# Attention, a gated MoE and a SwiGLU on one core: when the next stage's blocks are loaded and split, and when stores are issued

## The chip, the core and the metric

One core of one Trainium2 chip. The metric is the device time of one execution, in microseconds, as the median of several runs. TensorE is PE, VectorE is DVE, ScalarE is ACT, GpSimd is POOL; SP is the sync engine, whose queue issues nearly all of the DMAs here, strictly in program order: an entry that waits holds all entries behind it.

## The reference

Three parts follow one another; every output token depends on all three.

```python
k_p = k.reshape(B, H, Sp, 8, D).mean(3); v_p = ...           # B, H, S, D = 4, 8, 576, 64
attn = softmax(q @ k_p.T / sqrt(D)); x = (attn @ v_p)        # 2304 tokens x 512
p = domain_probs / domain_probs.sum(-1)
x = sum over e of p[:, e] * (relu(x @ w1[e]) @ w2[e])        # E = 4, 512 x 1024
xn = x / sqrt(mean(x * x) + 1e-6) * rms_g
out = (silu(xn @ w_gate) * (xn @ w_val)) @ w_out             # 512 x 1536
```

## The kernel before

The 2304 tokens are worked in three passes `p` of six tiles of 128 (TT = 6). A pass has an "m" part (4 experts x 4 rows of weights) and a "gv" part (6 rows of gate and value). The order is six **stages**: m0, m1, m2, then gv0, gv1, gv2; a stage of type m has 16 **quads**, one of type gv has 12 (`g`, `v` in turn). `quads` (L147) is the list, `stages` (L739) groups it, and `ids` are the quads of the stage in hand.

**A quad** (L286) multiplies the stage's x (512 x 768, cut in four blocks a11, a12, a21, a22 of 256 x 384) by a 2 x 2 block of weights with seven block products instead of eight (`STEPS`, L42). Each product is six matmuls: every float32 operand is split into a high part (an ACT copy to float32r) and a low part (a DVE subtraction), and high x high, high x low and low x high are added in PSUM (L304 to L306). X, Y and Z are the PSUM banks; after steps 0 to 2 ACT copies a bank away (`s`, L309), after steps 3 to 5 DVE adds (`u` L311 and L313, `v` L315). PE's next product into the same bank has to wait for that reader.

**x_ops** (L104) makes the seven operands of x for a stage: four DVE additions (L118), seven high parts on ACT (L111) and seven low parts on DVE (L115), into tiles `xo...` that have one buffer each, and so can be written only when the old stage's last quad has read them. `load_x` (L89) loads the four blocks from DRAM (`xs_d`), all at the end of the second-to-last quad (L822); `x_ops` is spread over the last quad from its step 2 on (L790) and over the first two steps of the new stage. For the early stages the blocks borrow the buffers `rw`, `tw`, `kr`, `vr`.

**The hook** (L776) runs after each step and hands out side work, in this order: the quad's own epilogue, a share of `second` (the second matmuls, L391: three matmuls a unit, two units a step in the m stages, one in the gv stages), the next quad's weights (`prep_w`, L175, and `prep_w2`, L227), `xit` (x_ops), `norms`, one piece of `convert_all` (L245), one entry of the attention's list (`att_step`). In the first stage and in gv0 the weights come raw, are combined on POOL (L193 to L197), split on ACT and DVE and stored to DRAM (`wr_d` L204, `wt_d` L212, `w2_d` L242); in later stages `prep_w` only loads them again (L186, L187). Raw blocks are loaded by `load_w` (L172) and `load_w2` (L224).

**norm** (L435) takes the MoE's result of a pass: for each of six tiles it loads y from DRAM (L449) into a buffer `st`, three steps later scales it (L453), two steps later transposes it on PE (L458), copies it to another `st` (L460), and stores it to `xs_d` (`store_x`, L87). `second` stores y with L420.

**Attention.** The first pass's six tiles come before the first quad, in the loop at L664 and in the order 0, 3, 1, 4, 2, 5: `att_a` is the scores (L556), maximum (L565), and eight exponentials on ACT (L568); `att_b` scales by the sums (L575 to L577); `att_c` transposes (L585) and copies to `aT` (L587); `att_d` multiplies by v (L599) and copies to x (L607). After every second tile `x_ops` runs on its part of x. The other tiles are handed out by steps during m0 and m1 (L712), the last of a stage ending at its step 95 of 112.

Of the kernel before, what the change touches and what calls it, by code (L numbers as in the profile page):

```python
# [53 lines left out]
def tile_kernel(ctx: ExitStack, tc, qp, kp, vp, dp, w1r, w2r, w64, rg, out):  # L54
# [34 lines left out]
    def load_x(kind, p, early):  # L89

        tags = (("rw", main), ("tw", main), ("kr", sba), ("vr", sba))
        for n, (o, d) in enumerate(((0, 0), (N, 0), (0, 1), (N, 1))):
            if early:
                tag, pool = tags[n]
                t = pool.tile([P, 4 * 256], F32, name="xr", tag=tag)[:, :2 * N]
            else:
                t = late["cv"].tile([P, 2 * N], F32, name="xr", tag=f"x{n}")
            t = t.rearrange("p (c n) -> p c n", c=2)
            nc.sync.dma_start(t, xs_d[kind, p, d, :, :, o:o + N])
            xr[o, d] = t  # L100

    xo = {}

    def x_ops(c0=0, c1=N, new=True):  # L104
# [16 lines left out]
        high("a11", a11)  # L121
        high("s3", a21)
        low("a11", a11)
# [13 lines left out]
        low("s1", a11)  # L137
        yield
        low("a12", a12)
        add(a12, a21, ALU.subtract)  # L140
# [23 lines left out]
    raw, wop = {}, {}  # L164

# [9 lines left out]
    def prep_w(i):  # L175
# [28 lines left out]
        nc.sync.dma_start(wr_d[n], wrf)  # L204
# [7 lines left out]
        nc.sync.dma_start(wt_d[n], wtf)  # L212
        yield
# [13 lines left out]
    def prep_w2(key):  # L227
        t = main.tile([P, 2, 2, DM], F32R, name="w2", tag="w2", bufs=4)
        w2[key] = t
        k, p, e, row = key  # L230
        d = w2_d[place2(k, e, row)]
        tf = f32(t).rearrange("p a s n -> p (a s n)")
        if p:
            nc.sync.dma_start(tf, d)
            return
        r = raw2.pop(key)
        for c in range(2):
            nc.scalar.activation(t[:, 0, c], r[:, c], AF.Copy)
            yield
            nc.vector.tensor_tensor(t[:, 1, c], r[:, c], f32(t[:, 0, c]), op=ALU.subtract)  # L240
            yield
        nc.sync.dma_start(d, tf)  # L242
# [148 lines left out]
    def second(keys, first, last):  # L391

        k, p, e, _ = keys[0]
        for t in (3, 4, 5, 0, 1, 2):
# [18 lines left out]
            elif k == "m":  # L413
                nc.vector.scalar_tensor_tensor(y_t[t], ps, gate, y_t[t], op0=ALU.mult, op1=ALU.add)  # L414
                if last:
# [4 lines left out]
                    nc.sync.dma_start(y_d[p, t], y_t[t])  # L420
# [14 lines left out]
    def norm(p):  # L435
# [10 lines left out]
        yield  # L446
        for t in range(TT):
            y = stage().rearrange("p d n -> p (d n)")
            nc.sync.dma_start(y, y_d[p, t])  # L449
            yield  # L450
            yield
            yield
# [7 lines left out]
            nc.scalar.activation(st, ps.rearrange("p (d n) -> p d n", d=ND), AF.Copy)  # L460
            store_x(1, p, t, st)
# [85 lines left out]
    def att_a(i):  # L547
# [5 lines left out]
        for j in range(NPAIR):  # L553
            o = (j % 2) * 2 * SP
            for p0, n, b in parts(i):
                nc.tensor.matmul(  # L556
                    sc[p0:p0 + n, j // 2, o:o + 2 * SP], q[:, j, p0:p0 + n],
                    kpb[b % 2][:, j].rearrange("p a s -> p (a s)"), start=True, stop=True,
                )
# [4 lines left out]
        scale = 1.0 / (POOL * math.sqrt(D))  # L564
        nc.vector.tensor_reduce(m.rearrange("p (a h) -> p a h", a=2), v, axis=AX.X, op=ALU.max)  # L565
# [5 lines left out]
        es_t[i] = es, sm  # L571

# [6 lines left out]
    def att_c(i):  # L579
# [6 lines left out]
        for a in range(2):  # L586
            nc.scalar.activation(aT[:, 4 * a:4 * a + 4, :], tr[a][:SP, :].rearrange("p (h s) -> p h s", h=4), AF.Copy)  # L587
# [56 lines left out]
    ]  # L644
    next(k0[0])
    next(k0[1])
    load_q(order[0])
# [16 lines left out]
    for n in range(TT + 2):  # L664
        if n >= 2:
            att_c(order[n - 2])
        if n < TT:
            att_a(order[n])
# [11 lines left out]
        if 1 <= n <= TT:  # L680
            att_b(order[n - 1])
# [85 lines left out]
    for si, ((moe, p), ids) in enumerate(stages):  # L767
        done = []
        for i in ids:
# [6 lines left out]
            def hook(n, u, v, x):  # L776
# [13 lines left out]
                if i != ids[-1] or n >= 2:  # L790
                    run(xit)
                run(norms)
# [8 lines left out]
            if i == ids[-1] and si + 1 < len(stages):  # L801
                xit.append(x_ops())
# [19 lines left out]
            if i == ids[-2] and si + 1 < len(stages):  # L822
                m2, p2 = stages[si + 1][0]
                load_x(0 if m2 else 1, p2, si < 2)
# [60 lines left out]
```

## Time and profile before

| | |
|---|---|
| median of 3 runs | 1359.64 us (1357.94 to 1361.63) |
| profiled execution, its own time | 1357.68 us |
| its span, first to last instruction | 1355.9 us |
| PE busy | 1273.2 us, 94% of the span |
| DVE, ACT, POOL busy | 782.8, 525.6, 255.0 us |
| mean granted TensorE clock | 0.982 |
| DMA moved | 323.37 MB, 238 GB/s over the span |

Busy time of PE is the union of matmul records, which overlap: a record of 0.34 us does not mean that the next begins 0.34 us later. The distance of two starts is the rate. An idle time in square brackets is the time in which the engine stood before an instruction, and the arrow names what ended it. Idle time of DVE, ACT and POOL costs nothing unless PE ends up waiting.

### The profile page before, as it was taken

The page shows a single profiled execution, that of the slowest core. Times are in us where ns is not written, and L with a number is a line of the kernel's source. Part 1 is how long each engine was busy: PE and PEld are TensorE (multiplying, and loading weights), DVE is VectorE, ACT ScalarE, POOL GpSimd, SP SyncE. Part 2 cuts the span into 40 slices and gives each one's busy share as a digit, 9 for nine tenths or more (in the row PEclk, how much of TensorE's full clock was granted, in tenths as well). Part 3 has the DMA queues.
Part 4 walks back from the last instruction along what each step waited for, and adds up shares of the span by engine and source line. Part 5 has one row for each costly group of instructions (what it writes and reads, how often), then busy time and mean ns, then how long its engine had stood idle before and what let it go on. Part 6 is the DMA issues. An engine that isn't in the chain of part 4 may idle for free.

```text
span 1355.9 us, 17501 instructions
## 1 busy us (share of the span) xinstructions
PE 1273.2 (94%) x6632; PEld 1142.7 (84%) x6632; DVE 782.8 (58%) x1265; ACT 525.6 (39%) x1165; POOL 255.0 (19%) x231
## 2 busy tenths in 40 slices
PE   4679999999999999999999999989988999989998
PEld 4569888888887889888888899878978899979997
DVE  3565666665556777746466653477567444464344
ACT  3656444444444333324423222356534233233321
POOL 5134324420012222310123220022220000000000
PEclk9789999999999999999999999999999999999999
DMA  7277777876778777774787774648867664646551
GB/s 211 63 273 265 257 259 255 291 253 251 257 256 290 260 276 264 262 274 151 290 291 271 268 253 171 233 171 307 302 245 256 233 240 194 261 164 227 225 225 47
DMA packets 87413, 323.37 MB, mean 238 GB/s; under 512 B 8736, under 2 KB 29216, under 8 KB 68128
## 3 DMA queue, kind: packets, MB, share of 16 engines
q1 hardware_dynamic: 86656, 319.89, 65.1%
q10 hardware_dynamic: 672, 2.36, 0.6%
q8 instruction: 52, 0.85, 0.3%
q14 instruction: 33, 0.27, 0.1%
HBM read 221.02 MB, written 101.19 MB: 238 GB/s over the span
## 4 chain that ended last, share of the span: by engine, by line
PE 56%; DVE 7%; DMA 5%; ACT 2%; issue 1%; SPq 0%; POOL 0%; ACTq 0%; DVEq 0%; POOLq 0%
PE py L402 8%; PE py L403 8%; PE py L401 8%; PE qX L304 6%; PE qX L305 6%; PE qX L306 6%; PE qY L304 3%; PE qY L305 3%; PE qY L306 3%; DMA cr<-w 2%; PE qZ L305 1%; PE qZ L306 1%; PE qZ L304 1%; DMA st<-y_d 1%; DVE xr L118 1%
## 5 line engine op out<-in xcount | busy, mean ns | idle before, releaser
L414 DVE SCALAR_TENSOR_TENSOR y<-py,dps,y 128x512 f32<-128x512 f32 x126 | 94.1, 747 | 123.0 <-PE py L403 123.0
L403 PE MATMUL py<-w,hB 128*128 128x512 f32 x396 | 157.8, 398 | 0.0
L402 PE MATMUL py<-w,hB 128*128 128x512 f32 x396 | 157.5, 398 | 0.0
L403 PE MATMUL py<-w,hA 128*128 128x512 f32 x396 | 157.1, 397 | 0.0
L402 PE MATMUL py<-w,hA 128*128 128x512 f32 x396 | 156.7, 396 | 0.0
L401 PE MATMUL py<-w,hB 128*128 128x512 f32 x396 | 155.3, 392 | 0.7 <-ACT st L460 0.7
L401 PE MATMUL py<-w,hA 128*128 128x512 f32 x396 | 154.2, 389 | 0.0
L309 ACT ACTIVATE s<-qX 128x384 f32<-128x384 f32 x168 | 82.6, 492 | 154.6 <-PE qX L306 154.4
L274 POOL TENSOR_TENSOR cx<-cx,ca 128x512 f32<-128x512 f32 x36 | 49.0, 1361 | 391.8 <-DVE ca L272 334.9
L304 PE MATMUL qX<-xos,wt 128*128 128x384 f32 x336 | 115.3, 343 | 6.2 <-ACT s L309 6.2
L305 PE MATMUL qX<-xos,wt 128*128 128x384 f32 x336 | 114.0, 339 | 0.0
L306 PE MATMUL qX<-xos,wt 128*128 128x384 f32 x336 | 113.5, 338 | 0.0
L311 DVE TENSOR_TENSOR u<-qY,s 128x384 f32<-128x384 f32 x84 | 46.6, 555 | 98.8 <-PE qY L306 93.8
L193 POOL TENSOR_TENSOR tw<-rw 128x512 f32<-128x512 f32 x28 | 44.3, 1581 | 315.2 <-DVE wt L210 229.2
L403 PEld LDWEIGHTS py<-w,hB 128*128 128x128 f32 x396 | 74.7, 189 | 16.2
L403 PEld LDWEIGHTS py<-w,hA 128*128 128x128 f32 x396 | 74.1, 187 | 16.1
L401 PEld LDWEIGHTS py<-w,hB 128*128 128x128 f32 x396 | 75.2, 190 | 8.3 <-ACT st L460 1.3
L402 PEld LDWEIGHTS py<-w,hB 128*128 128x128 f32 x396 | 74.9, 189 | 6.9
L401 PEld LDWEIGHTS py<-w,hA 128*128 128x128 f32 x396 | 74.4, 188 | 4.9
L329 ACT ACTIVATE hB<-u 128x768 fp32r<-128x768 f32 x48 | 40.7, 848 | 97.5 <-DVE u L313 97.4
L402 PEld LDWEIGHTS py<-w,hA 128*128 128x128 f32 x396 | 74.3, 188 | 4.9
L304 PEld LDWEIGHTS qX<-xos,wt 128*128 128x128 f32 x336 | 63.7, 189 | 16.7 <-ACT s L309 10.0
(143 smaller groups left out, 2968.2 us busy)
## 6 DMA issues: line engine op xcount, KB each, us to landing
wt<-wt_d SPq DMA_DIRECT2D x56, 1024.0 KB
w<-w_d SPq DMA_DIRECT2D x44, 1024.0 KB
wr<-wr_d SPq DMA_DIRECT2D x56, 768.0 KB
wt_d<-wt SPq DMA_DIRECT2D x28, 1024.0 KB
w_d<-w SPq DMA_DIRECT2D x22, 1024.0 KB
wr_d<-wr SPq DMA_DIRECT2D x28, 768.0 KB
cr<-w SPq DMA_DIRECT2D x36, 512.0 KB
wc_d<-cx SPq DMA_DIRECT2D x36, 256.0 KB
```

The costliest lines, as they stand in the source:

```text
L193: nc.gpsimd.tensor_tensor(t[:, T1:N3 + 1], r[:, B12:B12 + 1].to_broadcast([P, 2, 256]), r[:, B11:B22 + 1], op=sub)
L274: nc.gpsimd.tensor_tensor(x, x, m.bitcast(F32), op=ALU.mult)
L304: nc.tensor.matmul(bank[b], wh, xh, start=first and k == 0, stop=False, **kw)
L305: nc.tensor.matmul(bank[b], wh, xl, start=False, stop=False, **kw)
L306: nc.tensor.matmul(bank[b], wl, xh, start=False, stop=k == 1, **kw)
L309: nc.scalar.activation(s[n], bank[b], AF.Copy)
L311: nc.vector.tensor_tensor(u[:, 0], bank["Y"], s[2], op=ALU.add)
L329: nc.scalar.activation(h[:, 0], u, AF.Relu)
L401: nc.tensor.matmul(ps, lhs[0], w[:, 0, c], start=j == 0, stop=False)
L402: nc.tensor.matmul(ps, lhs[0], w[:, 1, c], start=False, stop=False)
L403: nc.tensor.matmul(ps, lhs[1], w[:, 0, c], start=False, stop=j == len(units) - 1)
L414: nc.vector.scalar_tensor_tensor(y_t[t], ps, gate, y_t[t], op0=ALU.mult, op1=ALU.add)
```

## The change

- `load_x` has two parts: three blocks (a11, a21, a22) are loaded at the end of the third-to-last quad, the fourth (a12) at the end of the second-to-last; the borrowed buffers become `kr`, `vr`, `aT`, `tw`, and a fifth tile (`rw`, or `x4`) holds a21 + a22.
- `next_x_ops` replaces `x_ops` between stages: its first subtraction is in the last step of the second-to-last quad, then a piece comes after every step of the last quad, and two in the new stage. A low part comes one step after its high part.
- `put` keeps a store of `wr_d`, `wt_d`, `w2_d` and `y_d` back; `tick`, once a step, issues it when it is due.
- `norm` loads y into a buffer of its own, the next tile's with the transposes of the tile before, and stores x two steps after the copy: nine steps a tile.
- The first attention tiles: q of the first tile is loaded ahead of k; in each round the scores of tile n come first, then the scaling of tile n-1, then the maximum of tile n, then `att_c` of n-1 (before: of n-2) and `att_d` of n-2; half of the copy to `aT` goes to DVE.

```diff
-    def load_x(kind, p, early):
-        tags = (("rw", main), ("tw", main), ("kr", sba), ("vr", sba))
-        for n, (o, d) in enumerate(((0, 0), (N, 0), (0, 1), (N, 1))):
+    def load_x(kind, p, early, part):
+        tags = (("kr", sba, 1152), ("vr", sba, 1024), ("aT", sba, 1024), ("tw", main, 1024))
+        for n, (o, d) in enumerate(((0, 0), (N, 0), (N, 1), (0, 1))):
+            if n // 3 != part:
+                continue
...
+        if part:
+            t = main.tile([P, 4 * 256], F32, name="xt", tag="rw") if early else late["cv"].tile([P, 2 * N], F32, name="xt", tag="x4")
+            xr["s2"] = t[:, :2 * N].rearrange("p (c n) -> p c n", c=2)
...
+    def next_x_ops():
...
+        tt(a21, a21, a11, op=ALU.subtract)
+        yield
+        a12, s2 = xr[0, 1], xr["s2"]
+        tt(s2, a21, a22, op=ALU.add)
+        high("a11", a11)
+        yield
+        low("a11", a11)
+        high("s3", a21)
+        yield
+        low("s3", a21)
+        tt(a11, a11, s2, op=ALU.add)
+        high("s2", s2)
+        yield
+        low("s2", s2)
+        high("a22", a22)
+        yield
+        low("a22", a22)
+        high("s1", a11)
+        yield
+        low("s1", a11)
+        high("a12", a12)
+        yield
+        low("a12", a12)
+        tt(a12, a12, s2, op=ALU.subtract)
+        yield
         high("s4", a12)
         yield
         low("s4", a12)
...
+    puts, clock = [], [0]
+    def put(dst, src):
+        puts.append((clock[0] + 2, dst, src))
+    def tick(end=False):
+        clock[0] += 1
+        while puts and (end or puts[0][0] <= clock[0]):
+            _, dst, src = puts.pop(0)
+            nc.sync.dma_start(dst, src)
...
-        nc.sync.dma_start(wr_d[n], wrf)
+        put(wr_d[n], wrf)
...
-        nc.sync.dma_start(wt_d[n], wtf)
-        yield
+        put(wt_d[n], wtf)
...
-        nc.sync.dma_start(d, tf)
+        put(d, tf)
...
-                    nc.sync.dma_start(y_d[p, t], y_t[t])
+                    put(y_d[p, t], y_t[t])
...
+        def load(t):
+            if t == TT:
+                return None
+            y = late["sb"].tile([P, DM], F32, name="yl", tag="yl")
+            nc.sync.dma_start(y, y_d[p, t])
+            return y
+        y = load(0)
         for t in range(TT):
-            y = stage().rearrange("p d n -> p (d n)")
-            nc.sync.dma_start(y, y_d[p, t])
-            yield
-            yield
-            yield
+            for _ in range(4):
+                yield
...
             nc.scalar.activation(st, ps.rearrange("p (d n) -> p d n", d=ND), AF.Copy)
+            y = load(t + 1)
+            yield
+            yield
             store_x(1, p, t, st)
...
+        if n:
+            att_b(order[n - 1])
         nc.vector.tensor_reduce(m.rearrange("p (a h) -> p a h", a=2), v, axis=AX.X, op=ALU.max)
...
+            if a and not at["few"]:
+                nc.vector.tensor_copy(aT[:, 4:], src)
+            else:
+                nc.scalar.activation(aT[:, 4 * a:4 * a + 4, :], src, AF.Copy)
...
+    load_q(order[0])
     next(k0[0])
     next(k0[1])
-    load_q(order[0])
...
     for n in range(TT + 2):
-        if n >= 2:
-            att_c(order[n - 2])
         if n < TT:
-            att_a(order[n])
+            att_a(order[n], n)
+        if 1 <= n <= TT:
+            att_c(order[n - 1])
...
-        if 1 <= n <= TT:
-            att_b(order[n - 1])
         if n >= 2:
             att_d(order[n - 2])
...
-                if i != ids[-1] or n >= 2:
+                if i != ids[-2] or n == 6:
                     run(xit)
+                tick()
                 run(norms)
...
-            if i == ids[-1] and si + 1 < len(stages):
-                xit.append(x_ops())
+            if i == ids[-2] and si + 1 < len(stages):
+                xit.append(next_x_ops())
...
-            if i == ids[-2] and si + 1 < len(stages):
+            if i in ids[-3:-1] and si + 1 < len(stages):
                 m2, p2 = stages[si + 1][0]
-                load_x(0 if m2 else 1, p2, si < 2)
+                load_x(0 if m2 else 1, p2, si < 2, int(i == ids[-2]))
```

## Rows read from the trace of the kernel before

**Rows 1.** PE's waits over the span: who waits, for whom, total us, times, longest

```profile
PE qX L304 <- DVE u L313: 17.8, 10, 4.8
PE qY L304 <- ACT s L309: 13.7, 7, 4.0
...
PE pt L458 <- DVE st L453: 6.7, 4, 4.3
PE qX L304 <- ACT s L309: 6.2, 6, 1.6
```

**Rows 2.** PE's waits in 318:346, in 870:893, in 1030:1056 (two), in 1183:1204 (two)

```profile
PE qX L304 <- DVE u L313: 3.1, 1, 3.1
...
PE qY L304 <- ACT s L309: 4.0, 1, 4.0
...
PE qX L304 <- DVE u L313: 4.1, 1, 4.1
PE qY L304 <- ACT s L309: 2.3, 1, 2.3
...
PE qY L304 <- ACT s L309: 3.1, 1, 3.1
PE qX L304 <- DVE u L313: 2.2, 1, 2.2
```

**Rows 3.** PE in order of time, undisturbed and after a wait: start, duration, instruction

```profile
703.37 0.33 PE L304 MATMUL qX<-xoa,wr 128*128 128x384 f32 x1
...
704.24 0.33 PE L306 MATMUL qX<-xoa,wr 128*128 128x384 f32 x1
...
705.80 0.33 PE L304 MATMUL qY<-xos,wt 128*128 128x384 f32 x1
...
1043.83 0.53 PE L304 MATMUL qX<-xos,wr 128*128 128x384 f32 x1
...
1046.07 0.53 PE L305 MATMUL qX<-xoa,wr 128*128 128x384 f32 x1
```

**Rows 4.** SP, DVE and ACT in order of time at gv0 to gv1

```profile
1031.01 3.39 SPq L99 DMA_DIRECT2D xr<-xs_d  x4
...
1037.64 0.96 DVE L118 TENSOR_TENSOR xr<-xr 128x768 f32<-128x768 f32 x1 [1.22 <-DMA xr<-xs_d]
...
1052.09 0.84 ACT L111 ACTIVATE xos<-xr 128x768 fp32r<-128x768 f32 x1 [4.45 <-DVE xr L118]
```

**Rows 5.** A stretch: length, busy PE, PEld, DVE, ACT, POOL, clock, DMA share, GB/s

```profile
1030.00:1056.00 26.00, 19.58 (x88) 17.95 (x87) 18.48 (x27) 11.05 (x18) 0.00 (x0) 0.88 0.75 274
```

**Rows 6.** SP and ACT in order of time in the second quad, and a stretch's busy times

```profile
82.14 0.33 SPq L212 DMA_DIRECT2D wt_d<-wt  x1
...
91.98 0.63 ACT L238 ACTIVATE w<-rw 128x512 fp32r<-128x512 f32 x1 [7.67 <-DMA rw<-w2r]
...
74.00:100.00 26.00, 19.04 (x101) 17.83 (x101) 18.05 (x27) 13.79 (x38) 9.03 (x10) 0.93 0.91 321
```

**Rows 7.** SP and DVE in order of time in `norm` of gv0

```profile
993.60 1.24 SPq L449 DMA_DIRECT2D st<-y_d  x1
...
1000.97 0.75 DVE L453 SCALAR_TENSOR_TENSOR st<-st,rs,g_bc 128x512 f32<-128x512 f32 x1 [6.33 <-DMA st<-y_d]
```

**Rows 8.** DVE, ACT and PE in order of time at the start

```profile
23.72 0.76 DVE L565 TENSOR_REDUCE m<-sc 128x8 f32<-128x576 f32 x1 [6.06 <-PE sc L556]
...
25.03 0.76 DVE L577 TENSOR_TENSOR es<-es,sm 128x576 f32<-128x576 f32 x1
...
31.32 0.32 ACT L568 ACTIVATE es<-sc,m 128x72 f32<-128x72 f32 x1 [2.86 <-DVE sm L576]
...
33.70 0.70 ACT L607 ACTIVATE stg<-av 128x256 f32<-128x256 f32 x2
...
37.70 0.32 ACT L568 ACTIVATE es<-sc,m 128x72 f32<-128x72 f32 x1 [2.36 <-DVE sm L575]
...
66.50 0.69 PE L304 MATMUL qX<-xoa,wr 128*128 128x384 f32 x1 [1.06 <-ACT xoa L111]
```

More of the change, by code (lines that the diff above doesn't have):

```diff
@@ L87, in store_x @@
             nc.sync.dma_start(xs_d[kind, p, d, :, :, t * P:(t + 1) * P], st[:, 2 * d:2 * d + 2])
-    def load_x(kind, p, early):
-        tags = (("rw", main), ("tw", main), ("kr", sba), ("vr", sba))
-        for n, (o, d) in enumerate(((0, 0), (N, 0), (0, 1), (N, 1))):
+    def load_x(kind, p, early, part):
[3 more added lines that the diff above has]
+                continue
             if early:
-                tag, pool = tags[n]
-                t = pool.tile([P, 4 * 256], F32, name="xr", tag=tag)[:, :2 * N]
+                tag, pool, size = tags[n]
+                t = pool.tile([P, size], F32, name="xr", tag=tag)[:, :2 * N]
             else:
@@ L121, in x_ops @@
         high("a11", a11)
+        low("a11", a11)
         high("s3", a21)
-        low("a11", a11)
         yield
@@ L137, in x_ops, with high, low @@
         low("s1", a11)
+        low("a12", a12)
+        add(a12, a21, ALU.subtract)
+        yield
+        high("s4", a12)
+        yield
+        low("s4", a12)
+        yield
+    def next_x_ops():
+        a11, a21, a22 = xr[0, 0], xr[N, 0], xr[N, 1]
+        tt = nc.vector.tensor_tensor
+        def high(name, src):
+            xo[name] = main.tile([P, 2, 2, N], F32R, name="xo" + name, tag="xo" + name)
+            nc.scalar.activation(xo[name][:, 0], src, AF.Copy)
+        def low(name, src):
+            t = xo[name]
+            tt(t[:, 1], src, f32(t[:, 0]), op=ALU.subtract)
+        tt(a21, a21, a11, op=ALU.subtract)
[4 more added lines that the diff above has]
+        yield
+        low("a11", a11)
+        high("s3", a21)
[12 more added lines that the diff above has]
+        high("a12", a12)
         yield
         low("a12", a12)
-        add(a12, a21, ALU.subtract)
+        tt(a12, a12, s2, op=ALU.subtract)
+        yield
         high("s4", a12)
@@ L460, in norm @@
             nc.scalar.activation(st, ps.rearrange("p (d n) -> p d n", d=ND), AF.Copy)
+            y = load(t + 1)
+            yield
+            yield
             store_x(1, p, t, st)
@@ L545, in pool_v, with att_a @@
         yield
-    def att_a(i):
+    def att_a(i, n=None):
         q = q_t.pop(i)
@@ L554, in att_a @@
             o = (j % 2) * 2 * SP
-            for p0, n, b in parts(i):
+            for p0, w, b in parts(i):
                 nc.tensor.matmul(
-                    sc[p0:p0 + n, j // 2, o:o + 2 * SP], q[:, j, p0:p0 + n],
+                    sc[p0:p0 + w, j // 2, o:o + 2 * SP], q[:, j, p0:p0 + w],
                     kpb[b % 2][:, j].rearrange("p a s -> p (a s)"), start=True, stop=True,
@@ L571, in att_a @@
         es_t[i] = es, sm
+        if n == TT - 1:
+            att_b(i)
     def att_b(i):
@@ L586, in att_c @@
         for a in range(2):
-            nc.scalar.activation(aT[:, 4 * a:4 * a + 4, :], tr[a][:SP, :].rearrange("p (h s) -> p h s", h=4), AF.Copy)
+            src = tr[a][:SP, :].rearrange("p (h s) -> p h s", h=4)
+            if a and not at["few"]:
+                nc.vector.tensor_copy(aT[:, 4:], src)
+            else:
+                nc.scalar.activation(aT[:, 4 * a:4 * a + 4, :], src, AF.Copy)
         aT_t[i] = aT
```

## The prediction

> **What bounds the kernel now.** I read four views in this order: what TensorE (PE) waited for over the span, the same view in stretches, the engines in order of time around its longest waits, and the start. PE is the bound: it has work nearly everywhere, and the time beyond its own work is the start and a few dozen waits. [rows 1] are the largest of these after the start: waits for a DVE add (`u`, L313), for ACT copies (`s`, L309), and for the normalised tile of `norm` (L453). The reader is to see that they are few and long: 4 waits make 6.7 us, and 10 make 17.8.
>
> Seven matmul steps make a quad; a step takes 2.43 us in stage m (703.37 to 705.80 in [rows 3], six matmuls and two units of `second`) and in the gv stages, with one unit less, an estimated 1.7; a quad so 12 to 17 us.
>
> The stretches show where the waits lie. [rows 2] has the waits at four of the five changes of stage: 3.1 at m0 to m1, 4.0 at m2 to gv0, 4.1 and 2.3 at gv0 to gv1, 2.2 and 3.1 at gv1 to gv2, 18.8 us in all. Behind such a wait the matmuls also go slower: in [rows 3] seven intervals take 2.24 us (0.32 each) after the 4.1 us wait, where five take 0.87 (0.174 each) in an undisturbed stretch (703.37 to 704.24). [...] After the 4.1 us wait twelve matmuls ran so (12 x 0.146 = 1.75 us). I count three more such spells at the changes, six to nine matmuls each, at the same price some 1.2 us each. So the changes cost 18.8 + 1.75 + 3.6 = 24.1 us.
>
> [rows 4] shows the cause. SP issues the four loads of the next stage's x at 1031.01, after everything that the quad before put on its queue; DVE starts `x_ops` at 1037.64, having waited for the transfer; then eleven wide operations of 0.96 us share DVE with the quad's own, most of them in five steps. ACT's in-order queue has its part of them between the copies that PE needs: at 1052.09 it had idled 4.45 us for a DVE subtraction, and PE's copy stands right behind.
>
> **The change part by part.**
>
> *x for the next stage (load_x, next_x_ops).* Eleven DVE and seven ACT operations remain, and four loads of 384 KB; nothing is saved but their place. Three blocks are loaded a quad earlier (12 us or more before their first use, against the 6.6 us from 1031.01 to 1037.64 in [rows 4]), the fourth a quad before its use. The first subtraction moves into the last step of the second-to-last quad, and the other ten DVE operations go over nine steps in place of seven; each high part is asked of ACT in the step in which PE has just read the old operand, and its low part of DVE one step later, so neither engine stands for the other. For the early stages the blocks go into the attention's `kr`, `vr`, `aT`; its last tile is read in step 95 of 112 and the load comes after step 97, so I cost that at nothing (uncovered, it is one landing, 6 us, of which a quad of 17 us hides all). What is late next: in the stretch of [rows 5] DVE was busy 18.48 us beside 19.58 of PE, so DVE can hardly keep ahead there, and the high part of `s4` in the new stage's first step still waits for the last subtraction. I leave 3 us at gv0 to gv1, where a tile of the longer `norm` now falls too, 1.5 at gv1 to gv2, and 0.5 at each of the two others: 5.5. Term: -24.1 + 5.5 = **-18.6**, between -24 and -10.
>
> *Stores late (put, tick).* No transfer is removed. SP runs its queue in order, so a store that waits for DVE holds the loads behind it, and a store issued first also goes first through the DMA engines. [rows 6]: in the second quad the store of `wt` is issued at 82.14 as DVE ends, that of `w2` next, then the load of the next raw `w2` block; it lands only at 91.98, ACT having idled 7.67 us, and PE's longest wait in [rows 1], 4.8, follows, with ten slow matmuls behind it (1.5). With both stores after the load, 2 MB no longer stand before it: at the 321 GB/s of this stretch they took 6 us. That is more than the wait, so it goes; the DMA engines stay full, and I leave 1.3. Term: 4.8 + 1.5 - 1.3 = **-5**, between 0 and -6.3. The buffers of `wr` and `wt` come free a step later, nine steps before they are written again: nothing. On SP a store now stands behind the loads of one more step (raw blocks, y, x), none of which reads what it writes.
>
> *y in norm.* [rows 7]: the load of a y tile was issued at 993.60 and its use began at 1000.97 after 6.33 us of DVE idle, for three steps of cover; PE stood 4.3 us, the largest of the four waits (6.7 us) in [rows 1]. Now the load is issued with the transposes of the tile before, seven steps ahead of its use, in a buffer of its own, and the store of x two steps after the copy it reads. Seven steps of 1.7 us are 12 us, over the 7.4 from 993.60 to 1000.97. The load waits on SP for the transposes that read its buffer, and behind it stand `convert_all`'s and the weights' loads; PE reaches the transposes in the step in which the load is issued, so nothing is held longer than that step. The loop takes nine steps a tile instead of six, which nothing needs sooner, save that at gv0 its last tile meets the x work (in the 3 us above). I leave 0.7: **-6**, between -7 and 0. [...]
>
> *Queue and order in stages m1 and m2.* What is left in [rows 1] after the changes, the second quad and `norm` is 17.8 - 9.4 - 4.8 = 3.6 for DVE, 13.7 - 9.4 = 4.3 for ACT's copy to Y, and 6.2 to X: 14 us, mostly ACT standing for `convert_all` or running eight exponentials. The x stores of `norm`, two steps later, no longer hold the weight loads on SP; the stores of `wc_d` and their landing remain. Bounds: half of it gone (-7), or the same meetings elsewhere with `norm` stretched (+4). I take **-2**, near the middle.
>
> *Start.* [rows 8]: from one tile's exponentials to the next is 6.4 us (31.32 to 37.70), of which the exponentials are 2.4 (to 33.70) and the chain on DVE 2.1 (23.72 to 25.79); the rest is transposes and scores on PE between the two. In the new order the scores come first and the scaling `att_b` before the maximum, so the period is exponentials plus DVE plus hand-overs, about 5.0. That gives 1.4 a tile for three tiles, 4.2. From the fourth on, the x pieces on DVE come before scaling and maximum, and ACT waits the scaling's 1.2 us more for two tiles: 2.4 back. The half copy on DVE lies beside exponentials. Loading q first ends PE's first wait, but the k blocks land that much later: 0.3 back, between -1 and +1.5. Term: **-1.5**, between -4 and +2, on the path, since the first quad starts only at 66.50.
>
> Sum: -18.6 - 5 - 6 - 2 - 1.5 = -33. The profiled execution took 1357.68 us, so 1324.6; the median of the runs shown is 1.96 above it: **1326**, cut to a whole number.
>
> **The rivals.**
>
> *The second wait at the changes stays.* DVE, filled to 18.48 of 19.58, lags over the stage's end, and ACT waits for the high part of `s4` as it did at 1052.09. Then 4.0 + 2.3 + 3.1 and their spells (some 3.6) remain, 13, of which 4.5 are already left in: 8.5 more, 1334.5. For it: the add and its high part are still one step apart. Against: the lag now builds up over more steps.
>
> *The DMA engines hold the loads anyway.* 91% busy in the second quad; a load issued early still queues, and the terms of stores and y go (11): 1337. For it: 6.33 us of idle at a load issued on time. Against: what stood before it were stores that now come after. [...]
>
> *The change does not do what it says.* A store falls due at clock + 2, but the same step's tick counts as one, so it leaves one step late. If DVE is further behind than that, SP is held as before and half of the store and m terms go: 1330.
>
> *Slower: early x loads hold SP.* The three loads after the third-to-last quad wait on SP for their buffers or for x stores, and the weight loads of the last quad stand behind them. They have a quad (up to 17 us) less a landing of 6 to spare; from a hold of 11 us PE stands one for one. A hold of 20 us at all five changes would give 5 x 9 = 45: 1371. Against: in [rows 4] the loads went out within 3.4 us, and what they wait for ends steps before.
>
> **How the numbers follow.** Forecast 0.60 (1326), second wait stays 0.18 (1334.5), DMA 0.11 (1337), one step only 0.06 (1330), SP held 0.05. Low end: nothing left at the changes (5.5), the start at -4 (2.5) and m1/m2 at -7 (5): 1313. High end: 1337 with the start at its worse bound (+3.5) and a us: 1342. Of the last case 0.03 is slower and 0.02 within 0.3% (a shorter hold); 0.3%, 4 us, is about what a measurement of this kernel tells from no change. The rest, 0.95, is faster.
>
> **What would show it.** Right: between 1025 and 1056 no wait of PE over 3 us, ACT's high parts spaced one a step, and no spell at 0.32; no idle before the y scaling on a transfer; the `w2` load of the second quad landing within 5 us; first quad at 65. Wrong: waits for `s` behind a high part in a stage's first quad, SP waiting over 10 us at the x loads, or first quad after 67.

## The result and the profile after

The changed kernel took **1317.95 us** (median of 4 runs, 1317.79 to 1321.71), the kernel before 1358.79 beside it (1357.33 to 1361.63): a ratio of 0.9704, with a 95% interval of 0.9680 to 0.9728. It is faster by 40.8 us, where 33 had been forecast; 1317.95 lies in the range of 1313 to 1342. The profiled execution took 1317.79 us, its span is 39.9 us shorter than before, and the work is the same: as many matmuls, 323.37 MB moved. Of all the runs below one is left out: undo_x once took 2080.24 us at a mean granted clock of 0.559.

The head of the page and its busy times, changed kernel:

```profile
span 1316.0 us, 17481 instructions
...
PE 1268.6 (96%) x6632; PEld 1140.0 (87%) x6632; DVE 782.8 (59%) x1271; ACT 521.1 (40%) x1159; POOL 254.2 (19%) x231
```

To see where the 39.9 us went I cut both traces at the same pieces of work: at PE's first matmul of the first quad (64.03 after, 66.50 before), and then around each change of stage, from the first matmul of the old stage's last quad to that of the new stage's second quad (of the third in m1 and m2). Between two changes lies the inside of a stage. The stretches of the changed kernel, in the columns of [rows 5] (length, then PE, PEld, DVE, ACT, POOL busy, granted clock, DMA share, GB/s):

```profile
64.03:310.99 246.96, 243.39 (x1296) 216.90 (x1297) 159.89 (x239) 120.88 (x292) 87.40 (x85) 0.98 0.76 272
310.99:358.52 47.53, 47.53 (x246) 42.90 (x244) 28.79 (x45) 22.02 (x54) 0.00 (x0) 1.00 0.76 280
358.52:588.38 229.86, 226.31 (x1246) 200.04 (x1245) 154.43 (x277) 85.59 (x213) 58.02 (x42) 1.00 0.74 267
588.38:634.05 45.67, 45.67 (x229) 41.17 (x228) 24.84 (x36) 17.82 (x34) 0.00 (x0) 1.00 0.57 217
634.05:845.94 211.89, 209.05 (x1046) 186.41 (x1045) 122.48 (x216) 60.58 (x110) 45.23 (x33) 1.00 0.74 268
845.94:876.65 30.71, 28.59 (x137) 25.52 (x135) 22.38 (x30) 16.36 (x28) 5.09 (x3) 0.94 0.35 129
876.65:999.72 123.07, 120.67 (x627) 110.56 (x626) 84.51 (x132) 66.84 (x121) 32.02 (x30) 1.00 0.77 283
999.72:1026.37 26.65, 24.29 (x120) 22.16 (x118) 22.13 (x32) 13.19 (x21) 0.00 (x0) 0.94 0.82 310
...
1143.81:1168.83 25.02, 22.30 (x116) 20.28 (x114) 19.70 (x28) 11.53 (x18) 0.00 (x0) 1.00 0.51 200
```

The stretches of the kernel before that answer to the last four of these:

```profile
864.74:898.54 33.80, 28.73 (x136) 25.31 (x135) 23.12 (x30) 16.50 (x28) 5.07 (x3) 0.95 0.30 101
898.54:1030.25 131.71, 123.17 (x632) 112.24 (x630) 85.38 (x133) 67.33 (x122) 32.11 (x30) 0.99 0.77 274
1030.25:1062.04 31.79, 25.37 (x116) 23.21 (x115) 21.73 (x31) 12.68 (x20) 0.00 (x0) 0.89 0.66 240
...
1179.47:1208.74 29.27, 24.05 (x115) 21.55 (x114) 19.84 (x28) 11.54 (x18) 0.00 (x0) 0.94 0.44 171
```

At gv0 to gv1 PE did the same work in 26.65 us instead of 31.79, and its idle time (length less PE busy) fell from 6.42 to 2.36. The insides of gv1 and gv2, where the change has next to nothing to do, are as long as before to 0.01 us. All stretches:

| stretch | before us | after us | difference | forecast |
|---|---|---|---|---|
| start, to the first quad | 66.50 | 64.03 | -2.5 | -1.5 |
| inside m0 | 252.75 | 246.96 | -5.8 | -5 |
| five changes of stage | 193.37 | 175.58 | -17.8 | -18.6 |
| inside m1 and m2 | 446.98 | 441.75 | -5.2 | -2 |
| inside gv0 | 131.71 | 123.07 | -8.6 | -6 |
| inside gv1, gv2, to the end | 264.59 | 264.59 | 0 | 0 |

What PE still waits for, over the span of the changed kernel (answers to [rows 1]):

```profile
PE tr L655 <- DVE es L647: 12.8, 6, 5.3
PE sc L622 <- ACT kpb L581: 9.8, 1, 9.8
PE qX L362 <- ACT s L367: 6.2, 7, 1.6
PE qX L362 <- DVE u L371: 4.4, 4, 1.8
PE qY L362 <- ACT s L367: 4.2, 3, 2.1
...
PE pt L521 <- DVE yl L516: 1.2, 3, 0.6
```

The two longest groups belong to the first attention tiles: all but 1.6 us of them lies ahead of the first quad. The waits for `u` have fallen from 17.8 to 4.4 us, those for the copies to Y from 13.7 to 4.2, those for the normalised tile from 6.7 to 1.2. Five of the waits that are left, 7.2 us (2.12; 1.77 and 0.58; 1.17 and 1.54), lie at the last three changes of stage, none at the first two.

SP's waits for `wt` in the kernel before:

```profile
SPq L212 <- DVE wt L210: 142.7, 26, 13.5
```

SP's waits in the changed kernel, and SP in order of time in the second quad (answers to [rows 6]):

```profile
SPq L282 <- DVE w L298: 107.7, 19, 9.8
...
SPq L222 <- DVE wt L269: 23.3, 6, 8.3
...
80.72 0.33 SPq L282 DMA_DIRECT2D rw<-w2r  x1
81.10 0.43 SPq L222 DMA_DIRECT2D wt_d<-wt  x1
81.58 0.43 SPq L222 DMA_DIRECT2D w_d<-w  x1
```

ACT at the use of that load:

```profile
85.26 0.64 ACT L296 ACTIVATE w<-rw 128x512 fp32r<-128x512 f32 x1 [2.98 <-DMA rw<-w2r]
```

The load of the raw `w2` block now stands ahead of both stores and is used 4.5 us after its issue (80.72 to 85.26); ACT used it at 91.98 before, and the 4.82 us wait of PE that followed is gone.

### The profile page after: what moved, and what is told of

Its sections match the earlier page's. It is cut to its first block, busy times and chain, and to the rows that moved or that the text cites. A ratio compares the mean times of both kernels' runs of the same rounds, so it can differ in the third digit from the quotient of the medians.

```text
span 1316.0 us, 17481 instructions
## 1 busy us (share of the span) xinstructions
PE 1268.6 (96%) x6632; PEld 1140.0 (87%) x6632; DVE 782.8 (59%) x1271; ACT 521.1 (40%) x1159; POOL 254.2 (19%) x231
## 2 busy tenths in 40 slices
DMA packets 87413, 323.37 MB, mean 246 GB/s; under 512 B 8736, under 2 KB 29216, under 8 KB 68128
## 3 DMA queue, kind: packets, MB, share of 16 engines
q1 hardware_dynamic: 86656, 319.89, 66.3%
q10 hardware_dynamic: 672, 2.36, 0.7%
## 4 chain that ended last, share of the span: by engine, by line
PE 80%; DVE 10%; DMA 4%; ACT 3%; issue 2%; POOL 1%; SPq 0%; ACTq 0%; DVEq 0%; POOLq 0%
PE py L460 12%; PE py L461 12%; PE py L459 12%; PE qX L362 8%; PE qX L363 8%; PE qX L364 8%; PE qY L362 4%; PE qY L363 4%; PE qY L364 4%; PE qZ L362 2%; PE qZ L363 2%; PE qZ L364 2%; DMA cr<-w 2%; ACT es L636 1%; PE tr L655 1%
```

## The experiments

Each kernel is the changed kernel with one edit (the two on POOL are s4_later with one more). The table has the timed result (median of 4 runs, of 3 for undo_x; ratio to the kernel before on the same chip, whose medians were 1357.45 to 1358.79 us) and, for the one profiled execution, by how much each stretch is longer than in the changed kernel's profile (us).

| run | median us | ratio, 95% interval | start | m0 | m0-m1 | m1 | m1-m2 | m2 | m2-gv0 | gv0 | gv0-gv1 | gv1-gv2 |
|---|---|---|---|---|---|---|---|---|---|---|---|---|
| undo_x | 1335.11 | 0.9833, 0.9795 to 0.9871 | 2.2 | 0.1 | 1.6 | -0.3 | 1.4 | 1.7 | 3.0 | 0 | 2.7 | 2.7 |
| x_early_only | 1333.60 | 0.9829, 0.9791 to 0.9868 | -0.3 | -0.1 | 1.6 | -0.4 | 1.4 | 3.1 | 4.2 | 0 | 4.3 | 2.7 |
| x_late_spread | 1322.17 | 0.9745, 0.9715 to 0.9774 | 2.3 | 0 | 3.2 | 0 | 0 | 0.6 | 0 | 0 | 1.0 | 0 |
| undo_put | 1325.06 | 0.9756, 0.9731 to 0.9781 | 0 | 6.6 | 0 | -0.2 | 0 | 0.7 | -1.5 | 0 | 1.5 | 0 |
| undo_norm | 1335.80 | 0.9829, 0.9800 to 0.9858 | 0.5 | -0.9 | 0 | 1.8 | 0 | 5.1 | 0.1 | 9.9 | 1.1 | 0 |
| norm_store_now | 1323.35 | 0.9755, 0.9712 to 0.9798 | 0.1 | 0.2 | 0 | 2.7 | 0 | 6.0 | -1.5 | 0 | 0 | 0 |
| s4_later | 1312.57 | 0.9677, 0.9631 to 0.9723 | -0.7 | 1.2 | 0 | 0.1 | 0 | 1.5 | -3.2 | 0 | -1.8 | -1.8 |
| s4_later_pool | 1314.30 | 0.9688, 0.9648 to 0.9728 | -0.1 | -0.9 | 0 | -0.2 | 0 | 0.2 | -3.2 | 0 | 0.7 | -1.8 |
| s4_pool_tail | 1315.30 | 0.9697, 0.9666 to 0.9728 | -0.8 | 0 | 0 | -0.4 | 0 | -0.6 | -3.5 | 0 | -0.9 | -0.9 |
| undo_start | 1320.77 | 0.9725, 0.9693 to 0.9758 | 0.9 | -0.9 | 0 | -0.3 | 0 | 2.7 | 0 | 0 | 1.6 | 0 |
| undo_order | 1318.71 | 0.9720, 0.9690 to 0.9751 | -0.3 | 0.3 | 0 | -1.1 | 0 | 2.4 | -1.5 | 0 | 1.5 | 0 |
| undo_q | 1320.58 | 0.9741, 0.9710 to 0.9772 | 2.5 | -0.3 | 0 | 0.3 | 0 | 0.3 | 0 | 0 | 0 | 0 |

Read it with care: undo_start and undo_order edit nothing after the start, and yet m2 and gv0 to gv1 differ by 2.7 and 1.6 us, m2 to gv0 by 1.5, m1 by 1.1. The profiled execution also lies up to 4.7 us from the median (s4_pool_tail, 1310.58 against 1315.30). A single stretch counts below only where it moved by more than that, or where a row shows the wait behind it.

### The next stage's x

**undo_x** puts the old `load_x` and the old order of operations back, between stages (`stage_x_ops` is the kernel before's `x_ops`).

```diff
-            if i in ids[-3:-1] and si + 1 < len(stages):
+            if i == ids[-2] and si + 1 < len(stages):
-                load_x(0 if m2 else 1, p2, si < 2, int(i == ids[-2]))
+                load_x(0 if m2 else 1, p2, si < 2)
-            if i == ids[-2] and si + 1 < len(stages):
-                xit.append(next_x_ops())
+            if i == ids[-1] and si + 1 < len(stages):
+                xit.append(stage_x_ops())
```

> The changed kernel with the old load_x and the old x_ops between the stages; all else as changed. Theory (each part buys what the two traces show at its place): the five changes of stage gave 17.8 us, so 1318 + 18 = 1336 us (1331 to 1340), with waits of PE of 2 to 4 us back at the changes of stage and none elsewhere. Rival (the late loads were held on SP by stores and by norm; with these out of the way the old place does as well): under 1324 us.

It took 1335.11 us, 17.2 over the changed kernel's median: the time that was expected, but not from the places that were expected. All five changes are longer, by 11.4 us together, not by the 17.8 that they lost: PE's waits there add up to 16.0 us, against 20.8 before and 7.2 in the changed kernel. For 4.8 of the 6.3 us that do not come back, at m0 to m1 and gv0 to gv1, the rows show a reason. DVE's first subtraction at m0 to m1, in the kernel before and in undo_x:

```profile
329.78 0.96 DVE L118 TENSOR_TENSOR xr<-xr 128x768 f32<-128x768 f32 x1 [2.28 <-DMA xr<-xs_d]
```

```profile
321.51 0.95 DVE L160 TENSOR_TENSOR xr<-xr 128x768 f32<-128x768 f32 x1
```

The kernel before waits for the transfer here and, for 1.22 us, at gv0 to gv1 [rows 4]; undo_x loads as late and waits at neither. At m0 to m1 its four loads no longer have two stores of weights ahead of them (before, stores at 318.40 and 319.16, x from 320.86 on; in undo_x, x from 313.51 on, the stores at 317.27 and 317.78). So the rival was right on this point, though not on the time: the late transfer is cured here by holding the stores back as well as by loading early, at gv0 to gv1 by that or by the new norm; undo_put and undo_norm, which load early, lose 0.0 and 1.2 us at the five changes. The remaining 1.5 us, at gv1 to gv2, are not explained.

**x_early_only** keeps the early loads and the fifth tile, and puts the old bunched order of operations back.

```diff
-            if i == ids[-2] and si + 1 < len(stages):
-                xit.append(next_x_ops())
+            if i == ids[-1] and si + 1 < len(stages):
+                xit.append(stage_x_ops())
-                if i != ids[-2] or n == 6:
+                if i != ids[-1] or n >= 2:
                     run(xit)
```

> The changed kernel with its early loads of x, but the old x_ops between the stages (bunched from step 2 of the last quad on). It parts the two halves of the x change. Theory (both count: late blocks make the first wait of a change of stage, bunched operations on DVE the second): half of what undoing both cost, 1318 + 8 = 1326 us (1323 to 1330), with waits for s in a stage's first quad still over 2 us. Rival one (only the loads were late): under 1321 us. Rival two (only the bunching counts): 1332 us or more, as with both undone.

1333.60 us, as slow as with the late loads, and rival two: early loads alone, with the stores held back, are worth nothing. PE's waits at gv0 to gv1, in order of time:

```profile
1020.94 0.45 PE L361 MATMUL qX<-xos,wr 128*128 128x384 f32 x1 [2.77 <-DVE u L370]
...
1031.38 0.45 PE L361 MATMUL qY<-xoa,wt 128*128 128x384 f32 x1 [2.30 <-ACT s L366]
```

and ACT at m2 to gv0:

```profile
875.24 0.84 ACT L158 ACTIVATE xos<-xr 128x768 fp32r<-128x768 f32 x1 [4.83 <-DVE xr L165]
875.99 0.47 ACT L366 ACTIVATE s<-qY 128x384 f32<-128x384 f32 x1
```

No transfer is late here, and ACT still stands 4.83 us for the last subtraction with the copy that PE needs behind it: DVE ran without a gap from 859.34 to 875.2. The bunching, not the landing, is the cause here.

**x_late_spread** is the opposite: all four loads late, the operations spread over the last quad.

```diff
         tt(a21, a21, a11, op=ALU.subtract)
-        yield
         a12, s2 = xr[0, 1], xr["s2"]
...
-                if i != ids[-2] or n == 6:
-                    run(xit)
+                run(xit)
...
-            if i in ids[-3:-1] and si + 1 < len(stages):
+            if i == ids[-2] and si + 1 < len(stages):
                 m2, p2 = stages[si + 1][0]
-                load_x(0 if m2 else 1, p2, si < 2, int(i == ids[-2]))
+                for part in range(2):
+                    load_x(0 if m2 else 1, p2, si < 2, part)
-            if i == ids[-2] and si + 1 < len(stages):
+            if i == ids[-1] and si + 1 < len(stages):
                 xit.append(next_x_ops())
```

> The changed kernel with all four blocks of x loaded at the end of the second-to-last quad, as before, and next_x_ops spread over the whole last quad (its first subtraction in that quad's first step). It is the other half of x_early_only, which showed that early loads alone give nothing. Theory (the spread is what pays, and the early load is what lets it begin in the first step): DVE stands some 5 us for the transfer in the first step of each last quad and PE part of it, 2 us at each of five changes: 1328 us (1324 to 1334). Rival (the spread alone pays; the wait for the transfer hides): under 1321 us.

1322.17 us, between the bounds of theory and rival: 13 of undo_x's 17.2 us come back with late loads. At m0 to m1, the one change that is clearly longer (3.2 us), DVE's first subtraction waits for the transfer:

```profile
321.19 0.96 DVE L164 TENSOR_TENSOR xr<-xr 128x768 f32<-128x768 f32 x1 [4.57 <-DMA xr<-xs_d]
```

PE's waits of 1.64 (for `u`) and 1.02 us (for `s`) follow it. At gv0 to gv1 DVE waits 2.10 us for the transfer, and PE's wait for `u` is 2.71 in place of 1.77. So the spreading carries this part, and the early loads are worth some 3 us at m0 to m1 and perhaps one at gv0 to gv1. (The 2.3 at the start is no effect of this edit: its start has the changed kernel's code.)

### The stores

**undo_put** issues every store at once.

```diff
     def put(dst, src):
-        puts.append((clock[0] + 2, dst, src))
+        nc.sync.dma_start(dst, src)
```

> The changed kernel with every store issued at once, as before. Theory: only the first quads lose, 5.8 us, and perhaps a us in m1 and m2: 1324 us (1322 to 1327), with ACT waiting over 5 us for the raw w2 block near 80 us and the quads after the sixth unmoved against each other. Rival (stores hold SP at the changes of stage and in gv0 too): 1330 us or more, with the loss spread over gv0 and the changes.

1325.06 us, 7.1 over the changed kernel, 6.6 of it inside m0. SP's waits and its order in the second quad:

```profile
SPq L216 <- DVE wt L269: 130.4, 27, 9.1
...
79.72 0.33 SPq L216 DMA_DIRECT2D wt_d<-wt  x1
80.32 0.32 SPq L216 DMA_DIRECT2D w_d<-w  x1
80.69 1.21 SPq L282 DMA_DIRECT2D rw<-w2r  x1
```

ACT at the use of the load:

```profile
89.78 0.63 ACT L296 ACTIVATE w<-rw 128x512 fp32r<-128x512 f32 x1 [7.90 <-DMA rw<-w2r]
```

The load is issued at the same time as in the changed kernel (80.69 and 80.72), and lands 4.5 us later, because two stores went to the DMA engines 1 us before it. PE's 4.50 us wait for `u` is back at 91.66. Here the order among the transfers counts, not the time at which SP could issue. SP's waits for `wt` (130.4 us, against 23.3 with the store held back and 142.7 before) cost PE next to nothing elsewhere.

### y in norm

**undo_norm** puts the old `norm` back.

```diff
-        y = load(0)
         for t in range(TT):
-            for _ in range(4):
-                yield
+            y = stage().rearrange("p d n -> p (d n)")
+            nc.sync.dma_start(y, y_d[p, t])
+            yield
+            yield
+            yield
...
-            y = load(t + 1)
-            yield
-            yield
             store_x(1, p, t, st)
```

> The changed kernel with the old norm: y loaded three steps ahead into st, x stored at once. Theory: gv0 loses its 8.6 us and m1 and m2 lose part of their 5.2: 1318 + 8.6 + 2 = 1329 us (1325 to 1332), with DVE waiting for y's transfer in gv0. Rival (with the stores of weights out of the way y lands in time): under 1321 us.

1335.80 us, 17.9 over the changed kernel and dearer than expected: 9.9 inside gv0, 6.9 in m1 and m2. DVE in gv0:

```profile
938.63 0.75 DVE L511 SCALAR_TENSOR_TENSOR st<-st,rs,g_bc 128x512 f32<-128x512 f32 x1 [4.21 <-DMA st<-y_d]
...
987.06 0.75 DVE L511 SCALAR_TENSOR_TENSOR st<-st,rs,g_bc 128x512 f32<-128x512 f32 x1 [6.55 <-DMA st<-y_d]
```

The second of these loads was issued at 977.97, so it took 9.1 us to its use with the loop's old three steps of cover; PE's waits for this tile are 7.7 us, 4 times. In the changed kernel no scaling waits for a transfer.

**norm_store_now** keeps the early load of y and issues the store of x at once.

```diff
             y = load(t + 1)
+            store_x(1, p, t, st)
             yield
             yield
-            store_x(1, p, t, st)
             yield
```

> The changed kernel with y loaded early as changed, but x stored right after its copy; nine steps a tile as before. Theory (in gv0 the early load was what counted, in m1 and m2 the store that no longer holds SP): gv0 keeps its gain, m1 and m2 lose 2 to 5 us: 1321 us (1319 to 1324). Rival (the held queue made y late in gv0 too): gv0 loses over 5 us and the whole is 1327 us or more.

1323.35 us. The inside of gv0 keeps its whole gain (0.0), so that is the early load of y; m1 and m2 lose 8.6, over twice what the two scatter together (1.1 and 2.7), so what they gained goes with the held-back store of x. (The medians differ by 5.4 us only; the profiled execution, 1325.23 us, is one of the longer ones.) SP's waits in this kernel have a group for it that the changed kernel's have not, and that the kernel before had (its line second):

```profile
SPq L87 <- ACT st L523: 9.9, 13, 3.3
```

```profile
SPq L87 <- ACT st L460: 52.6, 10, 10.7
```

A store asked for in the same step as the copy stops SP until ACT has made the copy, and loads stand behind it. PE's longest wait in 640 to 780 is 3.7 us here, 1.1 in the changed kernel. It is for a copy `s` that stands in ACT's queue behind `convert_all`, which waits for a store of its own to land; ACT here and in the changed kernel:

```profile
700.12 0.66 ACT L323 ACTIVATE cx<-cr 128x512 f32<-128x512 uint32 x1 [7.56 <-DMA wc_d<-cx]
```

```profile
693.58 0.67 ACT L323 ACTIVATE cx<-cr 128x512 f32<-128x512 uint32 x1 [4.97 <-DMA wc_d<-cx]
```

The same wait of PE is 2.2 us in undo_start and 1.8 in undo_order, whose norm is the changed kernel's; how much of the 3.7 belongs to the store of x is not shown.

### What is late next: the high part of s4

At gv0 to gv1 ACT stands for the last subtraction as it did in [rows 4], for 3.30 us, with PE's copy right behind (ACT, changed kernel, in order of time):

```profile
1017.96 0.85 ACT L158 ACTIVATE xos<-xr 128x768 fp32r<-128x768 f32 x1 [3.30 <-DVE xr L187]
1018.71 0.47 ACT L367 ACTIVATE s<-qY 128x384 f32<-128x384 f32 x1
```

**s4_later** asks for it one step later.

```diff
         tt(a12, a12, s2, op=ALU.subtract)
         yield
+        yield
         high("s4", a12)
```

> The changed kernel with one more step between the last subtraction of next_x_ops and the high part of s4, so that ACT's copy s of the new stage's second step no longer stands behind it. Theory (ACT's in-order queue makes the waits of 2.1, 0.6 and 1.5 us that are left in the first quads): they go with their slow spells, 4 us: 1314 us (1312 to 1316). Rival (DVE is what lags; PE then waits for u or for the low part of s4 in the last step instead): 1317 us or more.

ACT at m2 to gv0:

```profile
865.76 0.49 ACT L368 ACTIVATE s<-qY 128x384 f32<-128x384 f32 x1 [0.94 <-PE qY L365]
...
868.96 0.84 ACT L158 ACTIVATE xos<-xr 128x768 fp32r<-128x768 f32 x1 [1.98 <-DVE xr L187]
```

The copy now comes first. PE's wait of 2.12 us at m2 to gv0 is 0.36, that of 1.54 at gv1 to gv2 is gone, and the three late changes are 6.8 us shorter: some 3.3 of it are these two waits, most of the rest slow spells, which kernels that edit nothing there have or lack as well (last section). 1312.57 us is the lowest median of the study. Against the changed kernel the intervals of the ratios overlap (0.9631 to 0.9723 and 0.9680 to 0.9728), so that the waits are shown to go, and the 5 us between the medians are not shown by the timing.

**s4_later_pool** puts the first two additions on POOL as well.

```diff
-        tt(a21, a21, a11, op=ALU.subtract)
+        nc.gpsimd.tensor_tensor(a21, a21, a11, op=ALU.subtract)
...
-        tt(s2, a21, a22, op=ALU.add)
+        nc.gpsimd.tensor_tensor(s2, a21, a22, op=ALU.add)
```

> As s4_later, and the two first additions of next_x_ops (a21 - a11 and a21 + a22) on POOL, which is idle there. Theory (DVE lag makes the waits for u of 1.8 and 1.2 us in the last quads): two operations of 0.96 us less on DVE end them: 2 us below s4_later, 1312 us. Rival (POOL needs an estimated 2 us for each, from its 1.36 us for 512 columns, and is late itself, or slows DVE while it runs): as s4_later or above.

1314.30 us: no gain over s4_later. The waits for `u` stayed at 1.77 and 1.17 us, and a wait of 1.30 for the tile of `norm` came in: these two additions are not what makes `u` late.

**s4_pool_tail** takes s4_later and puts the third addition and the last subtraction on POOL.

```diff
-        tt(a11, a11, s2, op=ALU.add)
+        nc.gpsimd.tensor_tensor(a11, a11, s2, op=ALU.add)
...
-        tt(a12, a12, s2, op=ALU.subtract)
+        nc.gpsimd.tensor_tensor(a12, a12, s2, op=ALU.subtract)
+        yield
         yield
```

> As s4_later, with the addition into a11 (third step of the last quad) and the last subtraction on POOL instead of the first two. Theory (the waits for u of 1.77 and 1.17 us that s4_later and s4_later_pool both still have come from the two wide operations that DVE has in the third step, behind an accumulation that waits for PE): both waits under 0.5 us, 1310 us (1308 to 1312). Rival (POOL slows DVE or brings a11 late, so ACT stands for s1): the waits stay or s is waited for, 1313 us or more.

1315.30 us, as the rival has it. The waits for `u` fell to 0.90 and 0.30, so DVE's load in these steps does set them, but waits of 2.07 and 1.49 us for `s` took their place. POOL and ACT at gv0 to gv1:

```profile
1010.83 2.60 POOL L187 TENSOR_TENSOR xr<-xr,xt 128x768 f32<-128x768 f32 x1 [9.80 <-DVE xoa L162]
...
1013.46 0.84 ACT L158 ACTIVATE xos<-xr 128x768 fp32r<-128x768 f32 x1 [2.70 <-POOL xr L187]
1014.21 0.47 ACT L368 ACTIVATE s<-qX 128x384 f32<-128x384 f32 x1
```

The subtraction took 2.60 us on POOL here (the third addition, of the same size, 1.85 at 999.18), against 0.96 on DVE, and ACT's queue stood for it again.

### The start

**undo_start** has the old order of the first attention tiles and q behind k; **undo_order** the old order alone; **undo_q** q behind k alone.

```diff
-    load_q(order[0])
     next(k0[0])
     next(k0[1])
+    load_q(order[0])
...
+        if n >= 2:
+            att_c(order[n - 2])
         if n < TT:
-            att_a(order[n], n)
-        if 1 <= n <= TT:
-            att_c(order[n - 1])
+            att_a(order[n])
...
+        if 1 <= n <= TT:
+            att_b(order[n - 1])
```

(undo_start has both blocks and copies all of `aT` on ACT, undo_q the first block, undo_order the rest. undo_start and undo_order also have the old order inside `x_ops`: the changed kernel, besides what "The change" lists, makes the low part of a11 before the high part of s3 and the last subtraction a step earlier.)

> The changed kernel with the old first attention: q after k, old order of att_a to att_d, whole copy to aT on ACT, old order in x_ops. Theory: the first quad starts at 66.5 us again instead of 64.0, and nothing later moves: 1320.5 us (1319 to 1322). Rival (the early start is paid back in the second quad, where the DMA engines were full): 1318 us, with the second quad starting as in the changed kernel.

> The changed kernel with q first, but the old order of the first attention tiles, the old copy to aT and the old x_ops. Theory (the new order gains per tile early and gives most of it back at the x pieces, so q is the larger part): first quad within 1 us of the changed kernel. Rival (the order is the larger part): first quad 2 us later or more.

> The changed kernel with only the load of the first q behind the k blocks again. Theory (q first brought the first scores from 12.7 to 9.8 us and part of that reaches the first quad): first quad 1 to 2 us later than with q first. Rival (the exponentials and x pieces set the start): first quad within 0.5 us.

1320.77, 1318.71 and 1320.58 us: 2.8, 0.8 and 2.6 over the changed kernel, with intervals that all overlap its own. The first quad begins at 64.9, 63.8 and 66.6 us. These cannot be read as prices: in ten profiles of kernels with the changed kernel's own start it begins between 63.2 and 64.5 eight times and at 66.3 twice (undo_x, x_late_spread).

With q behind k the first scores come later (11.9 and 12.4 us, against 9.3 to 10.1), but in undo_q the third tile's exponentials begin only 0.4 us later than in the changed kernel (29.34 against 28.95). Its 2.5 us come with the fourth tile, where two operations of DVE are long; the second of them, in undo_q and in the changed kernel:

```profile
35.61 1.66 DVE L634 TENSOR_SCALAR m<-m 128x8 f32<-128x8 f32 x1
```

```profile
34.00 0.45 DVE L634 TENSOR_SCALAR m<-m 128x8 f32<-128x8 f32 x1
```

The scaling before it takes 1.54 us in place of 0.84. undo_x and x_late_spread have the same two long operations (1.54 and 1.66) with q first, and they are the two that begin at 66.3: the slip comes with q first too, and no price of q is shown. What lets it come or stay away is open. The old order of the tiles (undo_order) reaches the fourth tile's exponentials at 34.70 us and the first quad at 63.78, the new one at 34.55 and 64.03: no gain is seen.

## Why the prediction was right, and where it was not

**The changes of stage** (-18.6 forecast, -17.8 measured). The size held, the cause was only half read. I read in [rows 4] that the loads come late, and gave the gain to loads and spreading together; x_early_only shows that early loads alone give nothing, x_late_spread that late ones cost some 4 us, 3.2 of them at m0 to m1. What costs is eleven wide DVE operations (0.96 us each) in a few steps, with ACT's copies for PE queued behind them. The step "so neither engine stands for the other" failed for the last operand, as the forecast feared in the same part: the high part of `s4`, still one step behind its subtraction, was named as what is late next, and s4_later shows it. The amount left at m2 to gv0 was mis-sized: 0.5 was left in, the wait alone is 2.12, and PE's slow matmuls after it cost another 1.5. And undo_x gives back 11.4 us, not 18: the sum put the whole late landing down to early loads, where undo_x, with late loads, stands for no transfer. That the term came out so close is luck in part: 5.5 us were left in, and what is left is 7.2 of waits with two slow spells of some 1.5 each.

**The stores** (-5, measured -5.8 inside m0): right in place, cause and size. undo_put brings the `w2` load's late landing, PE's 4.5 us wait and 6.6 us back.

**y in norm** (-6, measured -8.6 inside gv0): right in cause, too small. I counted the waits of [rows 1] (6.7) alone. PE's idle time in gv0 fell by 6.1 (131.71 - 123.17 = 8.5 us to 123.07 - 120.67 = 2.4), and its busy time by 2.5 with the clock at 1.00 in place of 0.99: the matmuls that went slowly behind those waits were not in the sum, though I had charged them at the changes. One load of y took 9.1 us from issue to use in undo_norm; those in the changed kernel took 2.6 to 5.8 from issue to landing (L509):

```profile
DMA to landing us min/median/max: 2.6/3.2/5.8
```

**m1 and m2** (-2, measured -5.2): mis-sized. The term was taken near the middle of its bounds; norm_store_now loses 8.6 us there for the store of x alone. I had taken most of the 14 us of waits there for ACT's, standing for `convert_all` or running exponentials, and little for SP's; that the store of x no longer stops SP (52.6 us before) goes with about all that was gained. By which of PE's waits it does so is shown only in part.

**The start** (-1.5, measured -2.5): near by luck. The -2.5 is within what the same code scatters, and undo_start, with the old start of the attention, begins its first quad 1.6 us earlier than the kernel before (64.89 against 66.50). The step that failed is "1.4 a tile for three tiles": from the first tile's exponentials to the fourth's it is 20.86 us in the changed kernel and 21.07 in undo_order, 0.2 gained in place of 4.2. What the x pieces take back from there to the last tile's exponentials is 3.6 in place of 2.4 (17.39 against 13.82), and 3.2 us are gained behind those, which the sum had not. q ahead of k was booked at 0.3 the wrong way: the first scores came 2.9 us earlier (9.79 against 12.68), not later; by the third tile little of that is left.

**The rivals.** *The second wait stays*: it did in part, as PE's waits of 2.12, 0.58 and 1.54 for `s` behind a high part, 4.2 us in place of the 9.4 named. The 0.58, at gv0 to gv1, hides the size of the delay: a slow spell after the wait for `u` had held PE up by 1.5 us; in undo_put, undo_norm, undo_start and undo_order, without that spell, the wait for `s` there is 2.12 to 2.14. *The DMA engines hold the loads*: no; `w2` was used 4.5 us after its issue, and no scaling of y waited. *One step late only*: no, by what came of it: the terms of stores and m came in full. SP's waits for `wt` fell from 142.7 to 23.3 us, but SP is held elsewhere, 107.7 us before the load of the next raw `w2` block, until DVE has read the last one: that it is no longer held is not shown. *SP held by early x loads*: its longest wait at these loads is 2.8 us, against the 11 from which it would have cost.

Of the signs of being right, one failed: slow matmuls at a distance of 0.32 us were still there at m2 to gv0 and gv0 to gv1 (clock 0.94 in both stretches). One sign of being wrong came true beside the right total: the waits for `s` behind a high part in a stage's first quad.

## What to carry to other kernels

Where one in-order engine both feeds the next stage and frees the bound engine's banks, spread that stage's preparation one piece a step, and ask for a piece only when its source has had two steps (with the second step PE's wait of 2.12 us fell to 0.36). Early loads helped here only once the work behind them was spread (1335.11 to 1333.60 us bunched, 1322.17 to 1317.95 spread). On a queue that issues in order, as SP's does here, put stores that nobody awaits behind the loads that somebody does, by their order and not only by their time (the raw `w2` block: 4.5 us to its use ahead of two stores, 9.1 behind them).

## What the runs showed of the hardware

The same wait is not always followed by a spell at the lower clock. PE's wait for `s` at m2 to gv0 was 2.08 to 2.12 us in eight profiles; in five of them five or six matmuls of 384 columns after it ran at 0.32 us each, in three none. The stretch of 14 us around it in the changed kernel (columns as above):

```profile
866.00:880.00 14.00, 11.95 (x54) 11.06 (x55) 9.03 (x13) 8.12 (x15) 3.71 (x4) 0.88 0.44 170
```

and in undo_order, at the same place in the work:

```profile
867.34:881.34 14.00, 11.95 (x62) 11.10 (x63) 9.04 (x14) 9.39 (x18) 4.34 (x4) 1.00 0.52 207
```

In the same busy time undo_order ran 62 matmuls and the changed kernel 54, at a mean clock of 1.00 and 0.88; the change of stage is 1.5 us shorter, as in undo_put and norm_store_now, which do not edit it either. At gv0 to gv1 s4_later kept the 1.77 us wait and had no spell, so a part of its gain may be of this kind. What decides whether a spell follows such a wait is not shown.

The last subtraction of 128 x 768 float32 values took 0.96 us on DVE (median of five in the changed kernel) and, in s4_pool_tail at gv0 to gv1, 2.60 on POOL, the third addition there 1.85. The time of one transfer changed with what stood ahead of it: the raw `w2` block of the second quad was used 4.5 us after its issue where it went ahead of the two stores, and 9.1 (80.69 to 89.78) where they went 1 us ahead of it.
